# Decode attention on one core: a hardware loop over heads on TensorE, wide PV products, other buffers and finish

## The chip, the core and the metric

The kernel runs on one core of one Trainium2 chip. The metric is the device time of one execution in microseconds (us), as a median of several runs. The kernel before takes 651.89 us (3 runs, 650.51 to 652.79). All runs quoted here are of the state that the measurement calls fast.

## The reference

One query position attends to 65,536 keys; 32 query heads share 8 key/value heads, so K and V are 134 MB each and each is read once.

```python
B, Hq, Hkv, Sq, Sk, D = 1, 32, 8, 1, 65536, 128        # all bf16
def reference(q, k, v):
    k = jnp.repeat(k, 4, axis=1); v = jnp.repeat(v, 4, axis=1)
    scores = jnp.einsum("bhqd,bhkd->bhqk", q, k) * D ** -0.5
    p = softmax(scores, axis=-1)
    return jnp.einsum("bhqk,bhkd->bhqd", p, v)
```

## The kernel before

K and V are cut into 32 tiles each of 4 MB (128 partitions x 128 rows of 128 values); four tiles make one head. I call them K0 to K31 and V0 to V31. For each K tile DVE transposes eight groups of 16 rows, TensorE makes the scores (16 products of 16 columns per group), ACT moves them from PSUM to SBUF twice per tile, DVE takes the maximum. At the end of a head ACT takes the exponentials, and four tiles behind the K tiles TensorE multiplies the probabilities with V. The maximum waits for ACT, ACT waits for TensorE, and the next transposes come after the maximum in DVE's order.

```python
NK, NV = 2, 3                                     # K and V buffers
def values(i, tiles):                             # PV, 16 rows after each group of scores
    for t in tiles:
        ...
        if h < H - 1:                             # V is the weights, 4 columns are streamed
            ins = pe.matmul(pvb[h % 2][:, 0:R], lhsT=v_t, rhs=p_t, start=first, stop=final)
        else:                                     # last head: V is streamed, 128 columns
            ins = pe.matmul(pvb[h % 2][0:R, 0:D], lhsT=p_t, rhs=v_t, start=first, stop=final)
    if t == T - 1:
        ins.then_inc(pv_s, 1)
...
# loads, in order, on SyncE: K(i) waits for the transposes of K(i-NK),
sp.wait_ge(tr_s, (i - NK + 1) * G)
# V(i) waits for the product of V(i-NV)
sp.wait_ge(pv_s, i - NV + 1)
```

## Time and profile before

| reading | value |
|---|---|
| span of the profiled run | 651.0 us |
| K and V packets, share of 16 DMA engines (queue table) | 97.0% |
| instruction fetch (queue table) | 64 blocks of 16 KB, 0.6% |
| DMA rate from 26 to 490 us (busy time by windows) | 426 GB/s, DMA share 1.00 |
| from first transpose of a K tile to the next V load's issue | 13.5 us, 14.4 us at a head's first tile |

The page's row of DMA gives the mean busy share of 16 DMA engines in 40 equal slices of the span, in tenths (9 is 90% or more); PE is TensorE.

```profile
PE   0332144433334343344343343433443452444498
PEld 0322144432334333244342343422443352444498
DMA  9799999999999999999999999999999999999994
q8 instruction: 64, 1.05, 0.6%
```

DMA is busy from the second slice to the last but one, so the kernel is bound by loading. The Trainium skill (HBM Reference, Specifications (TRN2)) says that a core streaming alone measures about 425 GB/s, bounded by its DMA engines; the 426 GB/s above agree.

The groups of instructions: line, engine, operation, out<-in, sizes and count, then busy us and the mean ns of one, then idle us before them and what ended it.

```profile
L191 PE MATMUL pvb<-pts,vbuf 128*128 128x4 bf16 x3584 | 126.0, 166 | 16.0 <-ACT pts L343 15.8
L193 PE MATMUL pvb<-vbuf,pts 128*4 128x128 bf16 x512 | 31.3, 228 | 6.3 <-ACT pts L343 6.3
```

The last group: 512 products of 128 columns in 31.3 us are 61 ns each, and they keep TensorE busy from 617.6 to 648.96 us, past the last landing of V (near 644.4 us). They are the end of this kernel.

One K tile, K7, in order of time (start us, us, instructions, idle time before in brackets): its first transposes, TensorE's first two groups of 16 products, and the next V load, 13.5 us after the first transpose.

```profile
136.94 2.37 DVE L254 STREAM_TRANSPOSE ktb<-kbuf 128x1024 int32<-128x1024 int32 x2 [8.33 <-DMA kbuf<-in_k_dram]
138.33 0.58 PE L175 MATMUL qkb<-qblk,ktb 128*128 128x16 bf16 x16 [8.65 <-DVE ktb L254]
138.76 0.57 PE L191 MATMUL pvb<-pts,vbuf 128*128 128x4 bf16 x16
150.41 0.33 SPq L139 DMA_DIRECT2D vbuf<-in_v_dram  x1
```

### The profile page before, as it was taken

The numbers are of one execution on the slowest core, as the hardware profiler recorded it, in microseconds if no ns is written. First come the engines' busy times: TensorE is split into PE (matmuls) and PEld (weight loads), VectorE is DVE, ScalarE is ACT, GpSimd is POOL, SyncE is SP. The second block draws the span as 40 slices with busy tenths as digits, with TensorE's granted clock in tenths as the row PEclk, the third lists the DMA queues.
The fourth block names the chain that finished last, engine by engine and source line by source line (L and its number), as shares of the span: only waits on it lengthen the run. The fifth ranks groups of instructions, "written<-read, shape, count | busy, mean of one in ns | idle before, by whom it ended". The sixth has DMA issues, their size and how long they took to land.

```text
span 651.0 us, 18101 instructions
## 1 busy us (share of the span) xinstructions
PE 272.1 (42%) x8192; PEld 254.0 (39%) x8192; DVE 335.3 (52%) x356; ACT 263.6 (40%) x1098; POOL 7.4 (1%) x24
## 2 busy tenths in 40 slices
PE   0332144433334343344343343433443452444498
PEld 0322144432334333244342343422443352444498
DVE  2776445646346554356563466453655566666200
ACT  0454644235443263442723435424453255453600
POOL 0000000000000000000000000000000000000000
DMA  9799999999999999999999999999999999999994
GB/s 371 309 449 420 434 429 421 438 425 432 425 425 425 438 418 411 439 421 432 429 404 427 435 423 420 419 432 425 427 434 401 437 427 388 403 431 421 431 422 170
DMA packets 10668, 269.63 MB, mean 414 GB/s; under 512 B 1504, under 2 KB 1504, under 8 KB 2144
## 3 DMA queue, kind: packets, MB, share of 16 engines
q1 hardware_dynamic: 10232, 268.44, 97.0%
q8 instruction: 64, 1.05, 0.6%
q10 hardware_dynamic: 360, 0.04, 0.0%
q14 instruction: 12, 0.10, 0.0%
HBM read 268.47 MB, written 0.01 MB: 412 GB/s over the span
## 4 chain that ended last, share of the span: by engine, by line
DMA 49%; DVE 20%; ACT 16%; PE 9%; issue 4%; SPq 1%; POOL 0%; ACTq 0%; POOLq 0%; DVEq 0%
DMA kbuf<-in_k_dram 49%; DVE ktb L254 18%; ACT scs L329 13%; PE pvb L193 5%; PE qkb L175 3%; DVE hpart L262 2%; ACT pts L343 2%; PE pvb L191 1%; SPq L139 1%; POOL hmaxa L157 0%; ACTq L349 0%; DVE hmax L269 0%; ACT negb L334 0%; POOL qblk L146 0%; DVE olast L290 0%
## 5 line engine op out<-in xcount | busy, mean ns | idle before, releaser
L254 DVE STREAM_TRANSPOSE ktb<-kbuf 128x1024 int32<-128x1024 int32 x256 | 297.7, 1214 | 146.4 <-DMA kbuf<-in_k_dram 142.0
L329 ACT ACTIVATE scs<-qkb 32x64 f32<-32x64 f32 x1024 | 219.5, 214 | 340.1 <-PE qkb L175 328.9
L175 PE MATMUL qkb<-qblk,ktb 128*128 128x16 bf16 x4096 | 150.5, 175 | 354.6 <-DVE ktb L254 347.5
L175 PEld LDWEIGHTS qkb<-qblk,ktb 128*128 128x128 bf16 x4096 | 129.4, 105 | 371.7 <-issue 212.6
L191 PE MATMUL pvb<-pts,vbuf 128*128 128x4 bf16 x3584 | 126.0, 166 | 16.0 <-ACT pts L343 15.8
L191 PEld LDWEIGHTS pvb<-pts,vbuf 128*128 128x128 bf16 x3584 | 112.4, 104 | 16.7 <-ACT pts L343 16.5
L262 DVE TENSOR_REDUCE hpart<-scs 128x4 f32<-128x256 f32 x64 | 38.1, 595 | 122.3 <-ACT scs L329 122.3
L343 ACT ACTIVATE pts<-scs,negb 128x512 bf16<-128x512 f32 x32 | 40.9, 1430 | 0.3
L193 PE MATMUL pvb<-vbuf,pts 128*4 128x128 bf16 x512 | 31.3, 228 | 6.3 <-ACT pts L343 6.3
L193 PEld LDWEIGHTS pvb<-vbuf,pts 128*4 128x4 bf16 x512 | 31.2, 89 | 6.4 <-ACT pts L343 6.4
L290 DVE TENSOR_SCALAR olast<-pvb,rcol 4x128 bf16<-4x128 f32 x1 | 0.3, 337 | 30.6 <-PE pvb L193 30.6
L157 POOL PARTITION_ALL_REDUCE hmaxa<-hmax x8 | 3.0, 373 | 554.7 <-DVE hmax L269 554.7
L343 ACT ACTIVATION_READ_ACCUMULATOR pts<-scs,negb 128x1 f32 x32 | 8.1, 254 | 0.0
L334 ACT ACTIVATE negb<-hmaxa 128x4 f32<-128x4 f32 x8 | 1.6, 205 | 11.0 <-POOL hmaxa L157 11.0
L232 DVE STREAM_TRANSPOSE qt<-q 128x64 int32<-128x64 int32 x1 | 0.2, 245 | 8.2 <-DMA q<-in_q_dram 8.2
L276 DVE RECIPROCAL recip<-lsum 128x4 f32<-128x4 f32 x8 | 1.3, 168 | 5.9 <-POOL lsum L159 5.9
L159 POOL PARTITION_ALL_REDUCE lsum<-rsum x8 | 3.4, 430 | 43.9 <-ACT pts L343 43.9
L318 ACT ACT_TABLE_LOAD x1 | 1.3, 1283 | 2.6 <-issue 2.6
L269 DVE TENSOR_REDUCE hmax<-hpart 128x4 f32<-128x32 f32 x8 | 1.6, 206 | 0.3
L280 DVE TENSOR_TENSOR oT<-pvb,recip 128x4 bf16<-128x4 f32 x7 | 1.1, 161 | 0.2
L240 DVE COPY qblk<-qt 32x64 bf16<-32x64 bf16 x8 | 1.2, 182 | 0.1
L146 POOL MEMSET qblk<- 128x512 bf16 x1 | 0.5, 524 | 0.3 <-POOLq L367 0.3
(11 smaller groups left out, 1.4 us busy)
## 6 DMA issues: line engine op xcount, KB each, us to landing
kbuf<-in_k_dram SPq DMA_DIRECT2D x31, 4096.0 KB, 25.1
vbuf<-in_v_dram SPq DMA_DIRECT2D x31, 4096.0 KB, 16.3
kbuf<-in_k_dram SPq DMA_DIRECT2D x1, 2048.0 KB, 11.5
vbuf<-in_v_dram SPq DMA_DIRECT2D x1, 2048.0 KB, 11.9
kbuf<-in_k_dram SPq DMA_DIRECT2D x2, 512.0 KB, 4.5
kbuf<-in_k_dram SPq DMA_DIRECT2D x1, 1024.0 KB, 7.1
vbuf<-in_v_dram SPq DMA_DIRECT2D x1, 1024.0 KB, 14.0
vbuf<-in_v_dram SPq DMA_DIRECT2D x1, 512.0 KB, 14.8
```

What stands on the lines that cost most here:

```text
L139: sp.dma_start(vbuf[i % NV][:, :], src(vf, i)).then_inc(v_in[i % NV], 16)
L157: g.partition_all_reduce(hmaxa[:, hs], hmax[:, hs], P, bass.bass_isa.ReduceOp.max).then_inc(hma_s, 1)
L159: g.partition_all_reduce(lsum[:, hs], rsum[:, hs], P, bass.bass_isa.ReduceOp.add).then_inc(ls_s, 1)
L175: ins = pe.matmul(qkb[u % NQ][:, at:at + A * R], lhsT=kt[:, b, e, n * P:(n + 1) * P], rhs=qblk[:, qs:qs + A * R], start=be == 0, stop=be = ...
L191: ins = pe.matmul(pvb[h % 2][:, 0:R], lhsT=v_t, rhs=p_t, start=first, stop=final)
L193: ins = pe.matmul(pvb[h % 2][0:R, 0:D], lhsT=p_t, rhs=v_t, start=first, stop=final)
L254: dv.transpose(to.rearrange("p (b t j) -> p b t j", b=NB, t=TG), fr.rearrange("p (t b i) -> p b t i", b=NB, t=TG),).then_inc(tr_s, 1)
L262: dv.tensor_reduce(hp[:, h % 2, c, :], scs[h % 2][:, c * W:(c + 1) * W].rearrange("p (n g) -> p g n", g=R), AX.X, ALU.max,).then_inc(mx_s, 1)
L269: dv.tensor_reduce(hmax[:, h * R:(h + 1) * R], hp[:, h % 2, :, :].rearrange("p u g -> p g u"), AX.X, ALU.max,).then_inc(hm_s, 1)
L329: ins = ac.activation(to[a * S4:(a + 1) * S4, x, :, :], fr[x * S4:(x + 1) * S4, a, :, :], AF.Copy)
L334: ac.activation(negb[:, hs], hmaxa[:, hs], AF.Copy, scale=-scale).then_inc(nb_s, 1)
L343: ac.activation(pv[:, g_, :], sv[:, g_, :], AF.Exp, bias=negb[:, col], scale=scale, accum_out=rsum[:, col],).then_inc(ex_s, 1)
```

## The change

Its intent: fewer TensorE instructions (a loop over heads in place of written-out code, and 32 wide PV products per tile in place of 128), a third K buffer, one V buffer less, one buffer of probabilities instead of two with exponentials taken tile by tile, and sums and outputs made by TensorE in place of GpSimd and DVE.

```diff
-NK, NV = 2, 3
+J = 4
+NK, NV = 3, 2
 NKT = 4
-NQ = 6
+NQ = 4
-    pts = [sb(f"pts{i}", [P, TPH * R], DT.bfloat16) for i in range(2)]
+    pts = sb("pts", [P, TPH * R], DT.bfloat16)
 ...
+        for j in range(N + LAG):                  # LAG = 4; SyncE, in this order
+            if j < N:
+                load_k(j)
+            if j >= LAG:
+                load_v(j - LAG)
 ...
+            for m in quads:                       # 4 per group; 16 weights, 512 columns streamed
+                tau = c * T + m * J
+                ins = pe.matmul(
+                    acc[0:J * R, :], lhsT=pts[:, tau * R:(tau + J) * R], rhs=buf[:, m * J * D:(m + 1) * J * D],
+                    start=start and m == 0, stop=stop and m == T // J - 1,
+                )
 ...
+        with nc.Fori(0, loops, 1, ...) as it:     # 6 rounds, 4 K tiles in each
+            for c in range(C):
+                ...
+                for g in range(G):
+                    scores(j, g, it * (C * G) + (j * G + g + 1), ..., qcol)
+                    if g == 0:
+                        if c == 0:
+                            pe.wait_ge(ac_s, it * 2)
+                            pe.wait_ge(fin_s, it)
+                            sums()                               # column sums of the head before
+                            diagonal(fout, True, True).then_inc(fo_s, 1)   # 4 fp32 products: adds the 4 diagonal blocks
+                        pe.wait_ge(ex_s, it * (C * R) + (c + 1) * R)
+                        pe.wait_ge(v_in[c % NV], ...)
+                    values(vbuf[c % NV], c, range(g * QG, (g + 1) * QG), c == 0, c == C - 1)
```

In the wide product 4 query rows for 4 neighbouring V rows are 16 weights, and 512 columns of V are streamed; of the 16 x 512 results only the 4 diagonal blocks of 4 x 128 are wanted, and `diagonal` adds them. The last three V tiles go to freed K buffers, and the last V tile comes in five pieces, in products of 128 columns (into `acl`).

## The prediction

> **What bounds it now.** DMA. The 40-slice row has DMA at 9 from the second slice on; TensorE, DVE and ACT are 42%, 52% and 40% busy. By the queue table, K and V packets take 97.0% of 16 engines' 651 us = 631.6 us, instruction fetch 0.6% (64 blocks of 16 KB) = 4 us. The rest, from busy time in short windows: start 2 us; a hole at 22 to 26 us, 3.6 us (the third K load waits for the transposes of the first, 25.3 us); about 1.3 us of thin places at 490 to 550 us, where the load order changes; the end, where mean DMA work stops near 641.5. That end is TensorE: 512 PV products in a row from 617.6 to 648.96 (61.2 ns each), while the last V piece lands near 644.4. In between, a V tile plus a K tile takes 19.8 us of DMA; processing a K tile takes 13.5 us after landing, so some 6 us of queued loads remain at each new issue (timelines of SyncE and DVE).
>
> **What the change does.**
> 1. PV: 16 weight loads with 4-column products per group become 4 of 512 columns: about 4 x 0.23 = 0.9 us instead of 0.6 (estimate from 61 ns for 128 columns). Per tile 8 x (0.6+0.9) = 12 us < 19.8: off the critical path. The chain transpose, score, ACT move, maximum (7.2 us per half tile) lengthens by 0.4 us; slack falls to some 5 us.
> 2. Fewer TensorE instructions. The Trainium skill (Runtime: NRT & Kernel Launch, Instruction fetch mechanics) says that fetch goes in 16 KiB blocks and a branch outside the window fetches again; the trace has the blocks, no run yet shows the branch. I expect 17 to 45 blocks, saving 1 to 3 us of DMA.
> 3. Start: DVE waits neither for GpSimd nor for q: first transpose near 5.5 instead of 13.1 us; three K buffers close the hole at 22 us: -3.6. But V2 now waits for V0's product beside K5, not K4. Loads queued by then: K0 to K6, V0, V1 = 37.7 MB, gone at about 90.6 us. DVE pace (14.4 us a tile, about 5 us for the head's maximum, exponentials 5 us) brings K5's end to about 97: a new hole near 90 to 98 us, +7.5.
> 4. Exponentials by tile: 16 of 128 columns cost about what 4 of 512 did; hidden.
> 5. End: K31 comes five V tiles before the end, so TensorE keeps up with landings: after the last piece 8 products, 0.5 us of DVE, 2 us of output. -4. Between K31's and V28's load a hole under 1 us.
> 6. The irregular late load order is gone: -1.3.
>
> **Sum.** 651.9 - 3.6 + 7.5 - 2 - 4 - 1.3 + 0.7 = about 649. Most of the change lies off the critical path. Range 641 to 659. Faster by over 2%: 0.06; within 2%: 0.86; slower: 0.08.
>
> **What would show it.** Right: DMA row without a hole at 22 to 26 us and with one between 85 and 100, V2's issue at about 97; 428 GB/s between; span ending within 4 us after the last landing; the chain's last long step DMA of V, not PE; wide products 0.22 to 0.25 us apart. Wrong: V2 issued by 90 us (no hole: about 641), or DMA holes once per head.
>
> **What would make it wrong.** Dynamic addresses slowing score products (above 18 us per tile TensorE bounds), a refetch at every branch back beyond 5 us of slack, or the first head ending much earlier or later than reckoned.

## The result, and the profile after

The changed kernel takes 685.46 us (median of 4, 683.73 to 687.22); the kernel before took 652.34 us beside it. The ratio is 1.0509, with a 95% interval of 1.0471 to 1.0548: 5% slower, outside the range of the prediction. A ratio here is the mean time of one kernel's fast runs over that of the other's in the same rounds, so it is not quite the ratio of the medians quoted.

The page after has a new row, PEclk, the clock granted to TensorE in tenths of full speed; its mean is 0.838. The trace's clock records begin only at 92.68 us, and time without a record counts as full clock, so this mean is too high; more on that below.

```profile
PE   2232398466975657676766687756688566779778
PEclk9999997788787778888878887968868778878999
DMA  9999928999899999999999999799998999997993
q8 instruction: 17, 0.28, 0.2%
L191 PE MATMUL acc<-vbuf,pts 128*16 128x512 bf16 x928 | 291.2, 448 | 3.5 <-DMA vbuf<-in_v_dram 3.5
```

TensorE's row has doubled while its instructions fell from 8192 to 5306 products. The DMA row has one big hole in the sixth slice and several small ones. The instruction blocks fell from 64 to 17.

Here is TensorE in order of time at one K tile (start us, us, instructions, idle time before in brackets):

```profile
128.79 0.59 PE L179 MATMUL qkb<-qblk,ktb 128*128 x16 [9.08 <-DVE ktb L322]
129.31 1.88 PE L191 MATMUL acc<-vbuf,pts 128*16 128x512 bf16 x4
131.12 0.59 PE L179 MATMUL qkb<-qblk,ktb 128*128 x16
131.65 1.88 PE L191 MATMUL acc<-vbuf,pts 128*16 128x512 bf16 x4
133.45 0.58 PE L179 MATMUL qkb<-qblk,ktb 128*128 x16
133.96 1.03 PE L191 MATMUL acc<-vbuf,pts 128*16 128x512 bf16 x4
134.92 0.56 PE L179 MATMUL qkb<-qblk,ktb 128*128 x16
135.41 1.03 PE L191 MATMUL acc<-vbuf,pts 128*16 128x512 bf16 x4
```

After a wait of 9 us the same four wide products take 1.88 us, and some 5 us later 1.03 us. By the starts in the trace they follow each other at 427 ns or at 215 ns. The 16 score products of 16 columns hardly differ (0.59 and 0.56 us). The Trainium skill (TensorE: Matmul & The Clock Gate, Part 1) says that TensorE runs at half clock by default, that a busy window of about 3.4 us releases it, that an idle one throttles it again, and gives 426.7 and 215.7 ns for 512 columns; the spacings in this trace agree within 1 ns, and its clock records switch only at multiples of 3.41 us from the first.

From the same lines, a group of scores and wide products takes 2.33 us at half clock and 1.47 us at full clock. Half a tile is four groups, 9.3 or 5.9 us (estimates from these lines), while the chain through DVE and ACT took 7.2 us for half a tile before. So TensorE sets the pace of a half tile only at half clock.

What a slow TensorE does to loads: the first transpose of K9 starts at 167.65 us, and the next V load, which waits for the PV products beside K9, is issued at 188.63 us, 21.0 us later, instead of 13.5 us before the change. DMA has run dry by then. The same count at other tiles gives 16 to 21 us. At a tile that follows a head's end, as K9 does, the fp32 products of `diagonal` add 1.86 us at half clock, and DVE waits for them too. The loads at the first and at this later hole, with K9's first transposes between them:

```profile
65.18 0.33 SPq L124 DMA_DIRECT2D kbuf<-in_k_dram  x1
104.36 0.33 SPq L136 DMA_DIRECT2D vbuf<-in_v_dram  x1
...
164.69 0.43 SPq L124 DMA_DIRECT2D kbuf<-in_k_dram  x1
167.65 2.37 DVE L322 STREAM_TRANSPOSE ktb<-kbuf 128x1024 int32<-128x1024 int32 x2 [2.65 <-DMA kbuf<-in_k_dram]
188.63 0.33 SPq L136 DMA_DIRECT2D vbuf<-in_v_dram  x1
```

The first is the hole that the prediction saw coming, V2 behind V0's products; it is longer (104.4 instead of 97 us). The second kind was not foreseen, though "DMA holes once per head" stood among the signs that would show the prediction wrong. Busy time by windows (busy us and instructions of each engine, then granted clock, DMA share, GB/s) puts numbers on both. Before, then after:

```profile
22.00:26.00 4.00, 1.19 (x32) 1.01 (x32) 3.96 (x5) 0.39 (x3) 0.00 (x0) 1.00 0.14 37
26.00:490.00 464.00, 180.02 (x5760) 166.88 (x5760) 248.63 (x256) 198.46 (x832) 4.82 (x12) 1.00 1.00 426
641.00:651.00 10.00, 7.94 (x143) 7.76 (x139) 0.34 (x1) 0.00 (x0) 0.00 (x0) 1.00 0.09 31
```

```profile
88.00:106.00 18.00, 16.38 (x163) 6.82 (x162) 10.27 (x10) 9.01 (x41) 0.00 (x0) 0.82 0.24 87
106.00:634.00 528.00, 371.12 (x4206) 170.96 (x4205) 273.67 (x288) 228.03 (x1022) 2.22 (x6) 0.80 0.96 405
675.00:685.60 10.60, 8.31 (x139) 7.71 (x137) 1.18 (x3) 0.00 (x0) 0.00 (x0) 1.00 0.01 4
```

DMA time lost is window times (1 - share):

| idle DMA time, us | before | after |
|---|---|---|
| start, and the hole at 22 to 26 or at 88 to 106 | 1.3 + 3.4 | 0.9 + 13.7 |
| steady state | 2.1 | 21 |
| the end | 9.1 | 0.8 + 10.5 |
| sum | 15.9 | 47 |

The difference of 31 us is nearly all of the 34.6 us between the spans.

One reading of the page before must be corrected. Its windows say a clock of 1.00 everywhere, and so did I. But its trace has no record of the clock at all, and the last products of 128 columns tell another story. Two windows of TensorE (a product that reaches into a window is counted in it, so these counts are a few too high):

```profile
618.60:619.60 1.00, 1.00 (x13) 1.00 0.76 328
624.60:626.60 2.00, 2.00 (x40) 1.00 0.97 402
```

By the starts in the trace these products come 107 ns apart until 623.1 us, then 56 ns apart. So TensorE ran at half clock when that stretch began, while the column said 1.00; my 61 ns was a mean of two speeds, mostly of the fast one. The score products tell more. In the changed kernel the 16 of a group start 26.7 ns apart, in most groups, where the clock records say half, and 25.0 ns apart where they say full; in the kernel before they start 26.7 to 26.8 ns apart in all 256 groups. So, by this inference, the kernel before ran at half clock all along, up to this last stretch, and its products of 4 and 16 columns lost almost nothing by it. The change did not bring the half clock; it brought wide products that pay for it.

The clocks of the runs below have the same gap: the traces of e2, e9, e10 and e12 have no clock record at all, e6 has them only from 643 us on, and all others begin at 85 to 94 us. If TensorE was at half clock until the first record, the changed kernel's mean was about 0.77 and not 0.838 (an estimate).

### The profile page after: what moved, and what is told of

Its sections match the earlier page's. It is cut to its first block, busy times and chain, and to the rows that moved or that the text cites. A ratio compares the mean times of both kernels' runs of the same rounds, so it can differ in the third digit from the quotient of the medians.

```text
span 685.6 us, 12853 instructions
## 1 busy us (share of the span) xinstructions
PE 454.1 (66%) x5306; PEld 219.9 (32%) x5306; DVE 342.6 (50%) x371; ACT 289.6 (42%) x1290; POOL 4.4 (1%) x18
## 4 chain that ended last, share of the span: by engine, by line
DMA 47%; PE 26%; ACT 13%; DVE 10%; issue 2%; SPq 1%; POOL 0%; DVEq 0%; ACTq 0%
DMA kbuf<-in_k_dram 43%; PE acc L191 16%; ACT scs L407 13%; DVE ktb L322 8%; PE qkb L179 8%; DMA kbuf<-in_v_dram 5%; PE fout L203 1%; DVE hpart L330 1%; PE acl L282 1%; ACT pts L418 1%; SPq L136 1%; SPq L120 0%; PE acl L203 0%; PE fsum L199 0%; POOL hmaxa L163 0%
## 5 line engine op out<-in xcount | busy, mean ns | idle before, releaser
L179 PE MATMUL qkb<-qblk,ktb 128*128 (+1 forms) x4096 | 150.5, 173 | 219.9 <-DVE ktb L322 209.6
L191 PE MATMUL acc<-vbuf,pts 128*16 128x512 bf16 x928 | 291.2, 448 | 3.5 <-DMA vbuf<-in_v_dram 3.5
L191 PEld LDWEIGHTS acc<-vbuf,pts 128*16 128x16 bf16 x928 | 72.5, 96 | 97.2 <-issue 44.3
L418 ACT ACTIVATE pts<-scs,negb 128x128 bf16<-128x128 f32 x128 | 66.3, 570 | 0.4
L418 ACT ACTIVATION_READ_ACCUMULATOR pts<-scs,negb 128x1 f32 x128 | 23.9, 187 | 0.0
L191 PE MATMUL acc<-kbuf,pts 128*16 128x512 bf16 x64 | 15.6, 406 | 5.0 <-DMA kbuf<-in_v_dram 5.0
L203 PE MATMUL fout<-asb,ident 16*4 16x128 f32 x64 | 14.1, 390 | 0.0
L191 PEld LDWEIGHTS acc<-kbuf,pts 128*16 128x16 bf16 x64 | 5.9, 94 | 14.7 <-issue 8.0
L203 PEld LDWEIGHTS fout<-asb,ident 16*4 16x4 f32 x64 | 6.4, 108 | 4.2
L282 PE MATMUL acl<-kbuf,pts 128*4 128x128 bf16 x128 | 7.5, 219 | 0.0
L282 PEld LDWEIGHTS acl<-kbuf,pts 128*4 128x4 bf16 x128 | 7.2, 85 | 0.5 <-issue 0.2
```

Source lines behind the costliest of these rows:

```text
L179: ins = pe.matmul(qkb[u][:, at:at + A * R], lhsT=kt[:, b, e, n * P:(n + 1) * P], rhs=qcol(be), start=be == 0, stop=be == NB * NE - 1,)
L191: ins = pe.matmul(acc[0:J * R, :], lhsT=pts[:, tau * R:(tau + J) * R], rhs=buf[:, m * J * D:(m + 1) * J * D], start=start and m == 0, stop ...
L203: ins = pe.matmul(to[0:R, 0:D], lhsT=ident[:, j * R:(j + 1) * R], rhs=asb[:, j * D:(j + 1) * D], start=start and j == 0, stop=stop and j = ...
L282: ins = pe.matmul(acl[0:R, 0:D], lhsT=pts[:, tau * R:(tau + 1) * R], rhs=vhome(N - 1)[:, t * D:(t + 1) * D], start=t == 0, stop=t == T - 1,)
L418: ac.activation(pv[:, g_, :], sv[:, g_, :], AF.Exp, bias=negb[:, col], scale=scale, accum_out=rsum[:, at:at + 1],).then_inc(ex_s, 1)
```

## The experiments

Theory A: TensorE falls to half clock in each wait for a K tile; streamed columns then cost double, a tile takes 16 to 21 us instead of 13.5, and the queued loads (some 6 us before) do not last. Rivals: B, the load order, buffers or finish chain are at fault whatever the clock; C, the loop (register waits, dynamic addresses, branch back); D, products of 512 columns as such; E, an engine is simply the bound. All kernels gave correct results. "Before" below is the kernel before, run in the same rounds.

### e1: dummy products between tiles

```diff
+        def warm_up():
+            for _ in range(16):
+                pe.matmul(acl[0:J * R, :], lhsT=qblk[:, 0:J * R], rhs=qblk[:, :], start=True, stop=True)
 ...             # after each tile in the loop and in the written-out tail
+                warm_up()
```

> The changed kernel with 16 dummy products of 512 columns after each tile in the loop, so that TensorE idles less between tiles; nothing else differs. Theory A (TensorE drops to half clock in each wait for a K tile, and the wide products then take 450 instead of 240 ns, which eats the slack of the load queue): granted clock rises to 0.95 or more, the wide products run at about 240 ns, and the time falls to 645 to 667 us (the hole at 90 to 104 us stays). Theory B (load order or the chain at a head's first tile, whatever the clock): at least 680 us, since TensorE has only more to do.

Measured: 680.72 us (676.75 to 684.46), before 651.70; clock 0.919. That is outside what theory A was said to give and just inside what rival B was said to give (at least 680 us), though the time fell by some 5 us and the clock did not reach the 0.95 that A's case needed. TensorE in order of time shows why the clock did not stay up:

```profile
240.43 1.03 PE L191 MATMUL acc<-vbuf,pts 128*16 128x512 bf16 x4
243.14 0.57 PE L179 MATMUL qkb<-qblk,ktb 128*128 x16 [1.68 <-DVE ktb L329]
243.63 1.87 PE L191 MATMUL acc<-vbuf,pts 128*16 128x512 bf16 x4
```

After a pause of only 1.68 us inside a tile the products run at half clock again. The run was too weak a dose, and undecided.

### e2: the old form of the product, all else as changed

```diff
-            for m in quads: ...                          # 512 columns
+            for t in range(quads[0] * J, (quads[-1] + 1) * J):
+                ins = pe.matmul(
+                    acc[:, 0:R], lhsT=buf[:, t * D:(t + 1) * D], rhs=pts[:, tau * R:(tau + 1) * R], ...)
 ...             # diagonal(): one product, lhsT=asb (128x4), rhs=a 128x128 identity
```

> The changed kernel with the old form of the PV product (V as the weights, 4 columns streamed), and the output brought to rows by one product with a 128x128 identity; loop, buffers, load order and finish as in the change. Theory A (streamed columns at half clock cost the time): 644 to 656 us, V2 issued near 97 us, only the one hole of the prediction near 90 to 98 us. Theory B (load order, finish chain): at least 675 us. Theory C (loop): at least 675 us.

Measured: 659.74 us (658.56 to 660.85), before 651.70; 26 us faster than the change, 4 us above my range. After the first two PV tiles a tile takes 13.0 to 14.0 us again. The DMA row and two of its windows (this trace has no clock record, so its 1.00 says nothing; its score products start 26.7 ns apart, as at half clock):

```profile
DMA  9999959999999999999999999999999999999995
90.00:101.00 11.00, 7.10 (x224) 6.52 (x224) 8.92 (x9) 5.72 (x27) 0.00 (x0) 1.00 0.17 54
101.00:600.00 499.00, 209.05 (x6456) 190.21 (x6456) 264.68 (x284) 224.92 (x1008) 2.22 (x6) 1.00 1.00 423
```

The steady state has no holes left, with the loop, the load order and the finish of the change in place. B and C fall as causes of the steady loss. The hole at the first head stays, at 9.1 us (V2 issued at 99.9 us): this part does belong to the load order.

### e3: the loop written out

```diff
-        with nc.Fori(0, loops, 1, ...) as it:
+        for it in range(loops):
-                cols = [pe.snap(hq + be * A * R, ...) ...]
+                cols = [hq + be * A * R ...]
```

> The changed kernel with the hardware loop written out: same instructions, static addresses, no branch. Theory A (clock and streamed columns): 683 to 690 us, some 40 instead of 17 instruction blocks. Theory C (the loop's register waits, dynamic addresses or the branch back cost the time): below 670 us.

Measured: 694.75 us (692.90 to 695.28), 9 us slower than with the loop and 5 us above the range; 42 instruction blocks, clock 0.815. So the loop is no cost: with it the kernel is faster. By the 4 us that 64 blocks took before, 25 blocks more are some 1.6 us (an estimate from those two numbers); where the other 7 us come from I did not settle. The wide products were slower on average (461 instead of 448 ns), that is, more of them ran at half clock.

### e4: 128 columns and 4 weights

```diff
-J = 4
+J = 1
 ...             # acc is cut to its first J * D columns
```

> The changed kernel with J = 1: 128 products of 128 columns and 4 weights for each tile in place of 32 of 512 columns; the same number of streamed columns. Theory A (what counts is streamed columns at the granted clock): 680 to 692 us, 107 ns per product after a wait. Theory D (wide products of 512 columns themselves are the trouble, by blocking the queue or by power): below 670 us.

Measured: 693.52 us (689.14 to 698.05), 1.5 us above the range; clock 0.837. As many columns are streamed, in products a quarter as wide, and the time is no better (75 instruction blocks may account for part of the rest). D falls: the columns count, not the width.

### e5: K ahead of V in the queue of loads

```diff
         for j in range(N + LAG):
-            if j < N:
-                load_k(j)
+            if j == 0:
+                load_k(0)
+            if j + 1 < N:
+                load_k(j + 1)
             if j >= LAG:
                 load_v(j - LAG)
```

As changed, K(j) stands behind a V that waits for TensorE, so the third K buffer stays empty in the steady state.

> The changed kernel with one change in the order of loads: K tile j+1 is issued ahead of V tile j-4, so that the third K buffer is used in the steady state and some 10 us more of loads are queued. Theory A (slower processing of a tile at half clock eats the queued loads): the holes at heads' first tiles vanish, the hole near 90 to 104 us shrinks to 4 to 6 us, 650 to 662 us, with the granted clock as low as before. Rival E (TensorE or another engine is itself the bound, about 21 us per tile): at least 677 us.

Measured: 656.79 us (654.55 to 657.22), before 652.94, ratio 1.0053. Clock and DMA rows:

```profile
PEclk9999998867889877689786797877889877789799
DMA  9999998999999999999999999999999999976993
```

The clock is as low as ever (0.854), and yet 29 us have gone: with one more load queued, slow tiles no longer reach DMA, until the last slices. So a slow TensorE costs only where the queue is short, and E falls.

### e6: old form and K first

The edits of e2 and e5 together.

> The old form of the PV product in the changed kernel, and K tile j+1 issued ahead of V tile j-4. If the hole of 10 us near 90 to 100 us in the run with the old form comes from V2's wait standing ahead of K7 in the queue, it shrinks to 0 to 2 us; another 0 to 4 us may open between the loads of K31 and V28: 646 to 654 us. If the hole has another cause: 656 to 661 us as before.

Measured: 654.15 us (653.29 to 654.44), before 652.94, 0.15 us above the range. The hole near 90 to 100 us is gone (DMA share 1.00 from 90 to 100 us, 0.98 to 110); a new one opened at 570 to 610 us, 9.6 us by windows, larger than the 0 to 4 expected. There no K is left to load, and V26, V27 and V28 each wait for TensorE.

### e7: the kernel before, with V streamed in every head

```diff
-                if h < H - 1:
-                    ins = pe.matmul(pvb[h % 2][:, 0:R], lhsT=v_t, rhs=p_t, start=first, stop=final)
-                else:
-                    ins = pe.matmul(pvb[h % 2][0:R, 0:D], lhsT=p_t, rhs=v_t, start=first, stop=final)
+                ins = pe.matmul(pvb[h % 2][0:R, 0:D], lhsT=p_t, rhs=v_t, start=first, stop=final)
 ...             # each head scaled in rows, as the last head was
```

> The kernel before with one part of the change alone: V is streamed in every head (4 weights, 128 columns per product, as it did in the last head only), outputs scaled in rows as there; buffers, load order and no loop as before. Theory A: a tile takes 16 to 19 us instead of 13.5 to 14.4 us after its landing, holes open in the steady state, 658 to 680 us. Rival B/C (order, buffers, finish or loop are at fault): at most 654 us.

Measured: 689.57 us (685.51 to 692.33), before 652.94, ratio 1.0567. This one part of the change, done alone in the kernel before, costs as much as the whole change and 10 us more than I had expected; a tile takes 16 to 20 us. The trace shows where much of the rest is: from 560 to 600 us, in the irregular late order of loads, DMA's share is 0.77, a loss of 9.2 us. Its page:

```profile
PEclk9999998786778879577787887977779586758999
DMA  9899989999899998999999999799998997799995
L190 PE MATMUL pvb<-vbuf,pts 128*4 128x128 bf16 x4096 | 319.7, 243 | 18.4 <-ACT pts L335 18.3
```

### e8: more dummy products

```diff
                     values(vbuf[c % NV], c, range(g * QG, (g + 1) * QG), c == 0, c == C - 1)
+                    if g in (G - 3, G - 1):
+                        warm_up(6 if g == G - 3 else 26)
 ...             # the same in the written-out tail, but not after the last K tile
```

> The changed kernel with more dummy products than the first such run: 26 after each tile and 6 in the pause before a tile's group 6, where that run still fell to half clock. Theory A: granted clock over 0.96 in the steady state, wide products near 240 ns, a tile in 14.5 to 16.5 us, steady holes gone; the first hole (14 us) and the end stay: 660 to 672 us. If the clock rises and the time stays above 677 us, the clock is not the cause.

Measured: 668.65 us (668.11 to 670.68), before 652.94; clock 0.985 (0.98 from the first record, at 93 us, on). Adding work to TensorE (87% busy) made the changed kernel 17 us faster.

```profile
PEclk9999999999998999999999999999999999999799
DMA  9999948999999998999999999999999999996993
L191 PE MATMUL acc<-vbuf,pts 128*16 128x512 bf16 x928 | 243.8, 389 | 5.4 <-DMA vbuf<-in_v_dram 5.4
```

After its first two PV tiles a tile takes 14.7 to 17.6 us, and the holes left are the first one, one of some 2 us near 265 us, the one between K31 and V28 (6 us), and the end. The wide products' own spacing is 215 ns in nearly all cases (the mean of 389 ns above is a duration, from start to modelled end, and overlaps the next). Together with e2 and e7 this settles it for A: the clock, through streamed columns. The time is still 9 us above e2; how much of that is wide products at full clock and how much the dummy products was not separated.

### e9, e10, e11, e12: towards a version that is faster than both

e9 is e6 with the last V tiles in another order:

```diff
+        for i in (N - 3, N - 5, N - 2, N - 4, N - 1):    # V29, V27, V30, V28, V31
+            load_v(i)
```

> The old form of the PV product with K first, and the last V tiles loaded in the order V29, V27, V30, V28, V31, so that two loads into freed K buffers stand behind no wait for TensorE. The run before it lost about 9.6 us of DMA time at 570 to 610 us. If those are the waits of V26 to V28, they go: 642 to 647 us. If DMA was slow there for another reason: 652 to 655 us.

Measured: 658.46 us (656.82 to 658.89), before 653.17. A miss: 4 us slower than e6. The hole at 570 to 610 us did close (DMA share 0.99 to 1.04 there), so its cause was named rightly, but V28 now landed at 631 us, and TensorE, which takes V28 first, had four tiles to do after it.

e10 also takes the last V tile in the old form:

```diff
-                ins = pe.matmul(acl[0:R, 0:D], lhsT=pts[...], rhs=vhome(N - 1)[...], ...)   # 128 columns
+            values(vhome(N - 1), C - 1, range(a // J, b // J), False, True)
```

> The same, and the last V tile in the old form as well (128 weight loads, 4 columns) in place of 128 streamed columns, which in the last run took 4.6 us for the last 80 products at half clock. Theory A: another 2 to 5 us, 638 to 644 us, which is below the kernel before. If it gains under 1 us, the end was bound by landings.

Measured: 654.19 us (653.23 to 654.29), before 653.17: the step of 4 us came, the total did not, since e9's end was carried along. One thing in that expectation is wrong: 4.6 us for 80 products are 58 ns each, which is full clock, not half; only 32 of the 48 before them were slower. TensorE at the end:

```profile
633.33 3.55 PE L193 MATMUL acc<-pts,vbuf 128*128 128x4 bf16 x128 [14.97 <-DMA vbuf<-in_v_dram]
636.75 2.25 PE L193 MATMUL acc<-pts,kbuf 128*128 128x4 bf16 x79
640.73 3.55 PE L193 MATMUL acc<-pts,kbuf 128*128 128x4 bf16 x127 [1.73 <-issue]
644.45 4.95 PE L193 MATMUL acc<-pts,kbuf 128*128 128x4 bf16 x178 [0.17 <-issue]
```

e11 is the changed kernel, wide products and all, with only the orders of e9:

> The changed kernel with its wide products and its loop, only the order of loads changed: K first, and the same order of the last V tiles. Theory A with a queue deep enough to hide slow tiles: 644 to 651 us at a granted clock of 0.82 to 0.88, so the half clock costs nothing any more except at the end. If wide products still cost time in the steady state: 655 us or more.

Measured: 662.04 us (660.38 to 663.21), before 653.17: outside the range, and slower than e5 by 5 us. By the words of the expectation that would speak for a cost in the steady state, but DMA is whole there: from 500 to 630 us its share is 0.97 to 1.06 at clocks of 0.64 to 0.90, and the one hole before is of 3.6 us, at 100 to 110 us. So wide products cost nothing in the steady state; but with V28 late, V28 to V30 keep TensorE at wide products from 627.64 to 651 us, and the last tile follows.

e12 is e10 with V28 ahead of V30:

```diff
-        for i in (N - 3, N - 5, N - 2, N - 4, N - 1):
+        for i in (N - 3, N - 5, N - 4, N - 2, N - 1):    # V29, V27, V28, V30, V31
```

> The last run but one with one exchange at the end: V28 ahead of V30 in the queue. There V28 landed at 633 us, behind V30, and TensorE, which takes V28 first, had four tiles (about 14 us) left to do after it. When V28 was issued (602 us) V27 had not landed (611 us), so the queue is not dry without V30. If the late V28 is what kept the end: V28 lands near 622 us, TensorE keeps up with landings, 645 to 649 us, 1% below the kernel before. If the end is bound by the last landing near 641 us plus fixed work: 652 us or more.

Measured: 648.86 us (648.12 to 649.46), before 653.17; ratio 0.9931, 95% interval 0.9909 to 0.9953. This is faster than both kernels, by 0.7% against the kernel before.

```profile
DMA  9999999999999999999999999999999999999894
622.59 3.56 PE L193 MATMUL acc<-pts,vbuf 128*128 128x4 bf16 x128 [5.26 <-DMA vbuf<-in_v_dram]
```

V28 is there at 622.6 us, and the DMA row falls below 9 only near the end: windows of 5 us from 595 to 610 us lose some 3 us. 98.0% of the span is K, V and instruction packets (97.2% and 0.8%), which leaves little above the floor of loading.

## Why the prediction was wrong

1. *That DMA bounds the kernel before, and why the time moves only through holes in it*: right. The 31 us of new idle DMA time are nearly the whole loss.
2. *"4 x 0.23 = 0.9 us instead of 0.6 (estimate from 61 ns for 128 columns)", "off the critical path", "slack falls to some 5 us"*: this is the step that failed. The term was mis-sized by the clock: four wide products take 0.9 us at full clock, but 1.8 us after each wait for a K tile. A tile took 16 to 21 us instead of the 14 that I reckoned with, and the slack was gone: 21 us of holes in the steady state where I had none. Taking columns back (e2) removed them, streaming columns in the kernel before (e7) made them, keeping TensorE busy (e8) removed most. My 61 ns was a mean over 107 and 56 ns, and I took the clock to be full because the column said so.
3. *Instruction fetch, 17 to 45 blocks*: right at the edge, 17 blocks; by shares it went from 0.6% to 0.2% of the span, about 2.5 us of DMA.
4. *The start*: the old hole closed and V2 opened a new one, as told. It was 13.7 us instead of 7.5. With the old product (e2) it is 9.1 us, so the larger part is the load order and the rest went with the wide products. Its cause is shown by e6, where K first closes it.
5. *Exponentials, "cost about what 4 of 512 did"*: too low: 16 take 0.52 us each (starts 166.99 and 167.51 us), 8.3 us for a head, where 4 of 512 columns took 5.13 us (from 472.41 us on, before); but hidden, as e2 shows.
6. *The end, -4*: wrong; 11.3 us of idle DMA against 9.1. TensorE did not keep up with landings: the products of V30 ran from 666.6 to 675.1 us and those of V31 to 683.3 us.
7. *The late load order, -1.3*: cannot be told apart in holes of 21 us.

Left open: the 7 us of the written-out loop (e3) that instruction blocks do not explain; whether the late load order alone explains the 10 us that e7 lost beyond the range (9.2 us of holes lie there, but no run changed that order in e7).

## What to carry to other kernels

A matrix product with few streamed columns costs nearly the same at either clock of TensorE (here 26.7 or 25.0 ns for 16 columns), one with many costs double after a wait (427 or 215 ns for 512); so before streaming the large operand through an engine that idles for the DMA in every tile, cost the product at half clock, and do not read a clock of 1.00 from a trace that has no record of it. In a kernel bound by loads, ask of each tile how long it takes from its landing to the next issue, against the loads still queued; a load that waits for a late engine should not stand ahead of one that could go (here 29 us). Of the last loads, the one that is needed first should not come late (here 5 us).

## What the Trainium skill lacked or had wrong

- TensorE: Matmul & The Clock Gate, HAM oscillation: it gives the rule of no idle gaps over about 3.4 us. Here a pause of 1.68 us between busy stretches was followed by the half clock (e1: pause from 241.5 to 243.14 us, clock record of half from 243.53 us). With 6 dummy products in that pause and 26 after each tile the mean clock was 0.98 from the first record on (e8). The page's next section has shorter idle times that throttle too, but gives no length.
- The same page warns that clock records are unreliable. It lacks the case that there are none: in the kernel before, the column said 1.00 throughout while products of 128 columns came 107 ns apart for 5.5 us and then 56 ns apart. It has a floor for the spacing of small products, but does not say that they hide the clock, or how to read it from them: products of 16 columns started 26.7 ns apart at half clock and 25.0 ns apart at full clock.
- Runtime: NRT & Kernel Launch, Instruction fetch mechanics: it says that a branch to a target outside the current two pages fetches again, and that such loops are expensive. The loop here (1,280 products and weight loads by count of the program, and some register instructions and waits, run 6 times) was not fetched again: 17 blocks in all, 42 when written out (e3), and it was the faster by 9 us. With the old form of the product (over 2,048 instructions in the loop) it was: 75 blocks (e2). That fits the page's 2,048 instructions of TensorE's memory, not its two pages.
- No page that I used has a rule for the order of waits in one queue of loads; putting K ahead of V there was worth 29 us (e5), and exchanging two loads at the end 5 us (e12 against e10).
